# Chunk-selecting attention and a hardswish MLP on one core: the scheduler's slack, its mode charge and a new sequence of parts

## The chip, the cores and the metric

The kernel runs on one core of one Trainium2 chip. The metric is device time in microseconds of that core, from the first to the last instruction, as the median of several executions. The engines are PE (TensorE), DVE (VectorE), ACT (ScalarE), POOL (GpSimd) and SP (SyncE, which issues most of the DMA transfers).

## The reference, cut to what matters

```python
# attention: q, k, v are (4, 8, 768, 64) float32; chunks of 32 keys
k_min, k_max = min and max of k over each chunk
ub = sum_d max(q * k_min, q * k_max)           # an upper bound of the scores with a chunk
ub = where(causal chunk, ub, -1e9)
top = the 6 chunks with the largest ub, for each query
scores = where(in a top chunk and causal, q @ k.T / 8, -1e9)
attn = softmax(scores) @ v
# MLP on x = attn as (3072, 512); w_in (512, 2048), w_out (2048, 512)
h = x @ w_in
out = (h * clip(h + 3, 0, 6) / 6) @ w_out      # float32
```

## The kernel before

The attention is done for 16 pairs of heads, four pairs for each of the four batches. The MLP is done for 8 groups of 384 tokens, two for each batch. The work is cut into parts, each named by a token; one token often stands for an instruction group on PE and for what follows it on ACT or DVE:

- `k`, `q`, `v` (L281, L282, L290): loads of a pair's keys, queries and values. `w` (L302, L309): eight loads of quarters of the two weight matrices, issued by POOL. Each weight load waits for the cast of one pair's values, the pair that `WGATE` (L294) names, and for the weight load before it.
- `K`, `Q`: transposes of keys and queries on PE (L320), a copy out of PSUM on ACT (L335, L365), for keys the maximum and minimum over chunks on DVE (L339) and their difference (L347), for queries max(q, 0) on DVE (L369). `B`, `R`, `C`: casts to bf16 on POOL.
- `U`: the upper bounds on PE (L388) in 24 matmuls that use tiles of 64 x 32 of the array, and the addition of the causal bias on DVE (L396). `V`: their transpose (L410), the eight largest of each row (L418, twelve DVE instructions) and the comparison with the sixth (L421). `L`: the transpose of the selection (L438) and its copy out (L442).
- `S`, six for a pair: scores plus selection penalty on PE (L468, L473; tiles of 64 x 128), the exponential on ACT (L479) and the causal mask of the diagonal block on POOL (L483).
- `P`, two for a pair: probabilities times values on PE (L509), and the normalization on DVE (L514, L519).
- `X`: the attention's output transposed for the MLP; for batch 0 on PE (L557) with a DVE copy, for batches 1 to 3 by DMA transposes that SP issues (L546).
- `H`, eight for a group: eight matmuls with w_in (L578), relu on ACT (L582), minimum and product on DVE (L588). `O`: matmuls with w_out (L604, L625), a copy out on ACT (L610) and the store (L613).

The instructions are not written down in the order of these functions. The class `Plan` (L43) is a list scheduler that runs while the program is built. Each part has an engine, a duration, dependences and buffers in rings of fixed size. At each step every engine proposes one part (L95 to L108), the engine whose part starts earliest gets it, and the resulting order is the order in which all instructions are emitted. On the chip each engine then works through its own instructions in that order, so the planner's times matter only through the order that they give.

Two things decide what an engine proposes. The first is the time at which a part could start: the end of what it depends on plus a latency, or the time at which the engine is free, and on PE 0.095 us more (`SWITCH`) where the tile mode changes. Modes are 0 (whole array), 1 (`S`) and 2 (`U`). The second is the key of the part, its place in `SEQUENCE` (L134), where a lower place goes first:

```python
s = slack.get(eng, 0.0)
if mine is None or (at + s < mine[0]) or (at < mine[0] + s and op.key < mine[1].key):
    mine = (at, op)
```

With a slack of zero the second half of the condition is never true without the first, so the key has no say: the earliest part wins, and among equals the one that has been a candidate for longest. Before the change only PE has a slack, of 0.1 us (L686). The scores `S` of one pair also wait for all `S` of the pair before (L486), and PSUM allows three `S`, `H`, `K`, `Q` or `U` results at a time (ring `big`, L199).

Of the kernel before, what the change touches and what calls it, by code (L numbers as in the profile page):

```python
# [10 lines left out]
ACT = mybir.ActivationFunctionType  # L11
# [10 lines left out]

LAT = {"PE": 0.22, "DVE": 0.09, "ACT": 0.09, "POOL": 0.09, "LD": 2.0, "ST": 2.0}
SWITCH = 0.095


class Buf:
# [15 lines left out]
class Plan:  # L43
# [11 lines left out]
    def add(self, eng, dur, tok, fn=None, deps=(), take=(), use=(), chain=None, mode=0):  # L55
        deps = list(deps)
        if chain is not None:
            deps.append(self.last.get(chain))
        op = Op(eng, dur, tok, self.place(tok), fn, deps, take, use)
        op.mode = mode  # L60
        if chain is not None:
            self.last[chain] = op
        self.ops.append(op)
        return op
# [18 lines left out]
    def run(self, slack):  # L83
        cand = {}
        after = {}
        for op in self.ops:
            op.left = len(op.deps)
            for d in op.deps:
                after.setdefault(d, []).append(op)
            if not op.left:  # L90
                cand.setdefault(op.eng, []).append(op)
        order = []
        while any(cand.values()):
            best = None
            for eng, lst in cand.items():  # L95
                mine = None
                for op in lst:
                    r = self.ready(op)
                    if r is None:
                        continue  # L100
                    at = max(r, self.free[eng])
                    if eng == "PE" and op.mode != self.mode:
                        at += SWITCH
                    s = slack.get(eng, 0.0)
                    if mine is None or (at + s < mine[0]) or (at < mine[0] + s and op.key < mine[1].key):
                        mine = (at, op)
                if mine is not None and (best is None or mine[0] < best[0]):
                    best = mine  # L108
            if best is None:
                raise RuntimeError("no order")  # L110
            at, op = best
            cand[op.eng].remove(op)
            op.at, op.end = at, at + op.dur
            self.free[op.eng] = op.end
            if op.eng == "PE":
                self.mode = op.mode
            for b in op.take:
                b.slot = self.count[b.ring] % len(self.rings[b.ring])
                self.rings[b.ring][b.slot] = b
                self.count[b.ring] += 1  # L120
            for d in after.get(op, ()):
                d.left -= 1
                if not d.left:
                    cand.setdefault(d.eng, []).append(d)
            order.append(op)
        assert len(order) == len(self.ops)
        return order
# [4 lines left out]


SEQUENCE = """  # L134
H6.10 H7.14 Q10 H7.12 H7.4 P5.1 H3.6 P10.1 q15 P12.1 K9 S8.1 O6.1.8 v12 X7.2 O3.0.12 v0 H3.8 H6.14 q10 X3.2
S10.1 S11.1 K4 O3.0.4 R0 U4 L13 P10.0 U10 S9.0 P4.1 S6.4 S0.3 q14 L11 H6.0 Q15 O6.1.4 P9.1 Q5 O6.1.12 q0 v2
O3.2.0 S0.0 q2 P9.0 k10 H2.12 Q11 S5.1 V5 H7.0 S7.0 L0 X1.0 H2.14 V9 P8.0 K8 k14 H7.10 v9 H3.0 X2.1 H0.10 H3.4
v10 K0 q1 U3 S4.4 S13.1 R8 X3.1 R5 C7 H2.4 O1.2.12 C1 S0.5 S6.3 H2.10 O2.0.4 v13 K13 k1 K10 H6.12 B1 O6.0.12 R1
O4.1.0 O6.0.8 P6.0 H3.10 H1.14 X6.1 O7.0.8 O6.2.4 w5 H7.6 S12.0 V4 O6.0.0 O1.0.12 H0.14 O3.2.8 V10 B7 k9 Q14
O2.1.0 O4.2.8 H2.6 S9.3 R10 S8.5 P8.1 H0.6 S0.1 S2.1 L5 U0 H1.10 B3 S12.1 O1.0.8 K6 V2 U15 O3.1.4 C0 H1.12 K11  # L140
L4 P11.0 S0.4 S9.1 H0.0 k15 H4.0 O4.0.0 U2 Q2 P13.1 H0.2 w0 V12 H1.2 B4 U9 O0.0.12 H0.4 v3 O5.1.0 W0 S8.2 S10.2
Q8 X4.2 H0.12 H6.6 B9 O5.0.0 B15 k6 S2.2 L12 R3 P1.1 w6 X4.1 O1.1.12 O5.2.0 S7.2 k3 H6.4 W2 O4.0.12 q12 O4.1.12
q13 X3.0 S8.3 H3.12 L2 S11.4 v11 Q3 V1 S10.4 U5 O3.1.8 S14.5 O1.0.4 S6.2 L14 q7 C5 O7.1.12 k8 U8 k11 O4.1.8
O3.1.12 S14.0 O2.0.12 q8 S3.3 S6.0 Q12 Q1 S2.4 C13 P13.0 P7.0 S9.4 K1 H6.2 O1.2.4 v8 O1.1.8 V15 P15.1 O1.2.0 R12
H5.12 O5.1.12 H7.2 S5.0 v15 O2.0.8 O0.1.4 H2.2 X2.2 X1.2 X7.0 O7.1.8 k0 H2.0 R11 S11.0 S7.1 O7.2.12 B5 w7 H3.14
S1.3 S8.4 H7.8 X7.1 S14.3 S4.3 H4.8 S4.1 O4.0.4 S2.5 U6 B8 X5.2 S15.5 O2.2.0 k13 v6 S5.3 S7.5 q6 S8.0 S9.2 K15
v4 H1.8 H5.2 k2 q4 P0.1 U7 S5.4 v5 P7.1 O4.2.12 S6.5 v7 O3.1.0 O0.1.0 q5 P3.1 O1.2.8 O5.0.8 H0.8 S4.5 S7.4 S1.4
L7 V3 S3.1 O3.0.8 S1.1 V7 O0.1.12 S7.3 k7 B13 H5.10 S2.0 S3.0 P1.0 S11.5 U13 P11.1 O6.2.8 W1 V8 O4.2.4 P4.0 V13
S4.0 V11 O7.0.4 Q6 H2.8 B10 C15 k5 S13.0 X2.0 O0.0.0 U1 O2.2.8 U12 P6.1 O3.2.12 L8 L6 U14 O6.2.12 P14.0 S10.3 Q4
S5.5 S9.5 P2.0 K2 C8 w4 w3 O6.1.0 X6.2 V6 S14.1 O0.1.8 k4 S14.2 S10.0 R13 S6.1 U11 B12 P2.1 S5.2 O4.1.4 O3.0.0  # L150
S13.2 O2.1.8 P12.0 X5.1 C14 K12 O2.2.12 O2.1.12 L15 H1.6 H6.8 H3.2 L1 H5.0 K3 H4.4 V0 q11 H4.6 O2.1.4 v14 C6 L9
H4.10 O7.1.4 B6 S15.3 H4.2 C3 O6.2.0 S4.2 O7.2.0 H1.0 C10 O0.2.0 O7.1.0 X4.0 S0.2 C11 C2 B2 S11.3 O5.1.4 O4.0.8
w1 H5.14 S13.5 O6.0.4 P5.0 S10.5 S15.1 P14.1 O7.2.8 L3 K14 P0.0 H4.12 O5.1.8 R7 S12.4 S3.5 O2.0.0 S12.5 S12.3 R4
O0.0.4 K5 C9 S11.2 C12 O7.0.12 O4.2.0 S15.4 Q13 R9 R2 S12.2 O0.2.12 V14 O1.1.0 O3.2.4 S1.2 q3 X6.0 H4.14 R14 L10
B14 S3.2 R15 S3.4 B0 H1.4 X5.0 R6 q9 C4 Q0 S14.4 B11 w2 X0.0 v1 k12 H5.8 S1.5 H5.6 O1.1.4 O0.0.8 K7 P15.0 O0.2.4
O5.0.4 O5.2.4 S15.2 O5.2.8 S13.3 O1.0.0 S13.4 O0.2.8 S1.0 S15.0 O5.2.12 O2.2.4 O7.0.0 O5.0.12 Q9 H5.4 Q7 P3.0
S2.3 X0.2
"""
POS = {tok: n for n, tok in enumerate(SEQUENCE.split())}

# [6 lines left out]
def kernel(  # L167
# [21 lines left out]
    Q0 = TOPK * CH  # L189
# [11 lines left out]
    plan = Plan(rings, dict(PE=1.4, DVE=3.2, ACT=2.2, POOL=9.3, LD=0.3, ST=0.0), place)  # L201
    add = plan.add
# [88 lines left out]
                       take=[s["vs"]], chain="ldv")  # L291
        s["o_v"] = add("POOL", 0.86, f"C{i}", castv, deps=[s["ldv"]], take=[s["vb"]], use=[s["vs"]], chain="castv")

    WGATE = (0, 2, 1, 5, 6, 5, 6, 2)  # L294

    def plan_weights():
        wi = moe_w_in.rearrange("(k p) f -> p k f", p=P)
# [2 lines left out]
        for n in range(4):  # L300
            c = n * (DFF // 4)
            iss = add("POOL", 0.63, f"w{n}",  # L302
                      lambda c=c: nc.gpsimd.dma_start(WIN[:, :, c:c + DFF // 4], wi[:, :, c:c + DFF // 4]),
                      deps=[st[WGATE[n]]["o_v"]], chain="wi")
            iss.gate = n
# [13 lines left out]
        for j in range(NBLK):  # L319
            nc.tensor.transpose(T[:, j * P:(j + 1) * P], src.obj[:, j].rearrange("p e d -> p (e d)"), IDENT32[:])  # L320

    UDUR = 0.70

    def plan_K(i):
        s, tok = st[i], f"K{i}"
# [167 lines left out]
    norms = [[] for _ in range(B)]  # L493
# [39 lines left out]
    def plan_mlp(g, wdma):  # L533
        tok0 = g * GRP
        b = tok0 // S
        blk0 = (tok0 - b * S) // P
        xt, gt = Buf("xt"), Buf("gt")

        def do_xt():
            ops = []  # L540
            if b >= XDMA:
                for t in range(TPG):
                    def tr(t=t):
                        if t == 0:
                            new(xt, [P, TPG, KT_HID, P], BF16, "XT")
                        nc.sync.dma_start_transpose(xt.obj[:, t], xb[b].obj[:, blk0 + t, :])  # L546
                    ops.append(add("LD", 0.7, f"X{g}.{t}", tr, deps=norms[b] + ops[:1], take=[xt] if t == 0 else [],
                                   use=[xb[b]] if t == 0 else [xb[b], xt]))
                return ops
            for k0 in range(0, KT_HID, 2):  # L550
                ps = Buf("sm")

                def tr(k0=k0, ps=ps):
                    T = new(ps, [P, 2, GRP], BF16, "XTP")
                    for kk in range(2):
                        for t in range(TPG):
                            nc.tensor.transpose(T[:, kk, t * P:(t + 1) * P],  # L557
                                                xb[b].obj[:, blk0 + t, (k0 + kk) * P:(k0 + kk + 1) * P], IDENTB[:])

                def ev(k0=k0, ps=ps):  # L560
                    if k0 == 0:
                        new(xt, [P, TPG, KT_HID, P], BF16, "XT")
                    nc.vector.tensor_copy(xt.obj[:, :, k0:k0 + 2, :].rearrange("p t k s -> p k t s"),
                                          ps.obj[:].rearrange("p k (t s) -> p k t s", s=P))
                tok = f"X{g}.{k0}"
                o = add("PE", 0.35, tok, tr, deps=norms[b], take=[ps], use=[xb[b]], chain="XT")
                ops.append(add("DVE", 0.56, tok, ev, deps=[o] + ops[:1], take=[xt] if k0 == 0 else [],
                               use=[ps] if k0 == 0 else [ps, xt], chain="xev"))
            return ops
# [113 lines left out]
            plan_P(i, e)  # L683
    for b in range(B):
        plan_mlp_batch(b, wdma)
    order = plan.run(dict(PE=0.1))  # L686
    done_const = False
    for n, op in enumerate(order):
        if not done_const and op.eng not in ("LD",):
# [34 lines left out]
```

The softmax here doesn't subtract the row's maximum and nothing guards it: scores larger than these inputs give would overflow.

## Time and profile before

| | |
|---|---|
| time, median of three | 301.45 us (301.21 to 303.66) |
| span of the profiled execution | 300.2 us |
| busy share of ACT, DVE, POOL | 59%, 55%, 31% |
| mean granted clock of TensorE | 0.988 |
| moved by DMA | 32.20 MB, on average 107 GB/s |
| first matmul of the scores, of the MLP | 16.7 us, 60.5 us after the start |
| end of the last matmul to the end of the span | 3.8 us |

A line of the timeline gives the start, the time from the first start to the last end, the engine, the line of the code, what is written and read, and in square brackets idle time before it with what ended it. The ends of matmuls are modelled and overlap the next start, so durations on PE are best read from start to start.

### The profile page before, as it was taken

How to read it: one execution, taken by the hardware profiler on the slowest of the kernel's cores; microseconds unless marked ns; L12 is line 12 of the kernel's file. 1: busy time of each engine (PE TensorE's matmuls, PEld its weight loads, DVE VectorE, ACT ScalarE, POOL GpSimd, SP SyncE). 2: the span in 40 equal slices, each digit the busy share in tenths (PEclk: the TensorE clock that was granted, in tenths of full speed). 3: DMA queues.
4: the chain of work that ended last, by engine and by line, in shares of the span. 5: the costliest groups of instructions: out<-in, count | busy, mean ns of one | idle time of the engine just before them, and what ended most of it. 6: DMA issues, size and time to landing. Idle time of an engine off the chain costs nothing.

```text
span 300.2 us, 7214 instructions
## 1 busy us (share of the span) xinstructions
PE 287.3 (96%) x2948; PEld 178.4 (59%) x2970; DVE 163.6 (55%) x448; ACT 178.3 (59%) x219; POOL 92.5 (31%) x168
## 2 busy tenths in 40 slices
PE   7899999999999999999999999999999998999994
PEld 7657577765666556566555664566555654655444
DVE  4768887756669876236857461468421551625300
ACT  1557798987556358755766772565567832654311
POOL 8756776662106135531220342021133100000000
PEclk9959999999999999999999999999999999999999
DMA  9999999999507999762400005201011015001112
GB/s 172 218 185 217 203 210 193 220 196 198 89 0 184 243 228 206 156 134 68 107 35 3 35 12 130 72 0 37 13 60 37 2 31 144 2 1 71 37 70 71
DMA packets 92914, 32.20 MB, mean 107 GB/s; under 512 B 85584, under 2 KB 89936, under 8 KB 92880
## 3 DMA queue, kind: packets, MB, share of 16 engines
q1 hardware_dynamic: 87088, 27.14, 42.1%
q0 software_dynamic: 4224, 4.19, 8.8%
q10 hardware_dynamic: 1568, 0.39, 0.7%
q8 instruction: 23, 0.38, 0.6%
q14 instruction: 11, 0.09, 0.1%
HBM read 27.26 MB, written 6.29 MB: 112 GB/s over the span
## 4 chain that ended last, share of the span: by engine, by line
PE 82%; DVE 4%; ACT 4%; DMA 3%; SPq 2%; issue 2%; POOL 1%; ACTq 0%; DVEq 0%; POOLq 0%
PE HP L578 28%; PE OP L604 22%; PE PVP L509 8%; PE SPS L468 7%; PE SPS L473 5%; PE UBP L388 4%; PE QT L320 3%; PE KT L320 3%; ACT PT L479 2%; PE UBQ L410 2%; SPq L546 2%; DMA XT<-Xb 2%; DMA KS<-in_k_dram 1%; PE OP L625 1%; PE SLT L438 1%
## 5 line engine op out<-in xcount | busy, mean ns | idle before, releaser
L479 ACT ACTIVATE PT<-SPS 128x1024 bf16<-128x1024 f32 (+1 forms) x96 | 82.3, 924 | 18.7 <-PE SPS L473 15.2
L588 DVE SCALAR_TENSOR_TENSOR GT<-U,HP 128x768 bf16<-128x768 bf16 x64 | 60.8, 953 | 54.4 <-ACT U L582 49.3
L578 PE MATMUL HP<-XT,WIN 128*128 128x384 bf16 x512 | 86.0, 326 | 1.4 <-DMA XT<-Xb 1.0
L604 PE MATMUL OP<-WOUT,GT 128*128 128x512 bf16 x346 | 82.6, 379 | 1.6 <-issue 0.3
L582 ACT ACTIVATE U<-HP,THREE 128x768 bf16<-128x768 f32 x64 | 57.7, 901 | 33.4 <-PE HP L578 33.2
L578 PEld LDWEIGHTS <-WIN 128*128 128x128 bf16 x512 | 49.4, 98 | 35.1 <-issue 2.2
L483 POOL TENSOR_SCALAR_AFFINE_SELECT PT<-PT 128x256 bf16<-128x256 bf16 x96 | 38.6, 408 | 73.5 <-ACT PT L479 72.9
L604 PEld LDWEIGHTS <-GT 128*128 128x128 bf16 x368 | 34.4, 98 | 39.1 <-issue 1.7
L610 ACT ACTIVATE OT<-OP 128x512 f32<-128x512 f32 x23 | 13.7, 597 | 45.4 <-PE OP L604 43.6
L468 PE MATMUL SPS<-RHS,LHS 64*128 64x512 bf16 (+3 forms) x256 | 34.5, 315 | 1.4 <-ACT PT L479 1.3
L473 PE MATMUL SPS<-SELT,EM 64*128 64x288 bf16 (+6 forms) x384 | 32.8, 253 | 0.2 <-DVE SELT L442 0.2
L509 PEld LDWEIGHTS <-PT 128*128 128x128 bf16 x672 | 23.3, 98 | 4.5 <-issue 1.5
L473 PEld LDWEIGHTS <-EM 64*128 64x128 bf16 x384 | 18.9, 96 | 8.1 <-issue 1.1
L375 POOL CAST RHS<-QTS 128x768 bf16<-128x768 f32 x16 | 15.1, 951 | 26.7 <-ACT QTS L365 26.1
L514 DVE RECIPROCAL RINV<-PVP 128x6 f32<-128x6 f32 x32 | 6.1, 192 | 30.5 <-PE PVP L509 30.3
L468 PEld LDWEIGHTS <-LHS 64*128 64x128 bf16 x256 | 11.7, 95 | 14.2 <-issue 10.7
L354 POOL CAST LHS<-KTS 128x768 bf16<-128x768 f32 x15 | 12.6, 847 | 23.0 <-ACT KTS L335 22.8
L519 DVE TENSOR_TENSOR Xb<-PVP,RINV 128x384 bf16<-128x384 f32 x32 | 17.7, 555 | 0.9
L365 ACT COPY QTS<-QT 128x768 f32<-128x768 f32 x16 | 12.4, 802 | 6.6 <-PE QT L320 5.1
L339 DVE TENSOR_REDUCE KM<-KTS 128x24 f32<-128x768 f32 x15 | 13.9, 943 | 4.4 <-ACT KTS L335 4.3
L335 ACT COPY KTS<-KT 128x768 f32<-128x768 f32 x15 | 11.9, 807 | 5.2 <-PE KT L320 5.2
L320 PE MATMUL KT<-IDENT_114,KS 128*128 128x128 f32 x96 | 13.5, 284 | 0.5 <-DMA KS<-in_k_dram 0.3
(113 smaller groups left out, 233.6 us busy)
## 6 DMA issues: line engine op xcount, KB each, us to landing
VS<-in_v_dram SPq DMA_DIRECT2D x32, 192.0 KB, 4.6
KS<-in_k_dram SPq DMA_DIRECT2D x31, 192.0 KB, 4.5
QS<-in_q_dram SPq DMA_DIRECT2D x31, 192.0 KB, 4.5
out_dram<-OT SPq DMA_DIRECT2D x23, 256.0 KB, 2.0
WIN<-in_moe_w_in_dram POOLq DMA_DIRECT2D x4, 512.0 KB, 7.2
WOUT<-in_moe_w_out_dram POOLq DMA_DIRECT2D x4, 512.0 KB, 10.9
XT<-Xb SPq DMA_TRANSPOSE x18, 2.5
out_dram<-OT SPq DMA_DIRECT2D x2, 128.0 KB, 1.7
```

Of the source, the lines that this page charges most:

```text
L320: nc.tensor.transpose(T[:, j * P:(j + 1) * P], src.obj[:, j].rearrange("p e d -> p (e d)"), IDENT32[:])
L375: nc.gpsimd.tensor_copy(new(s["rhs"], [P, S], BF16, "RHS")[:], qts.obj[:])
L468: nc.tensor.matmul(T[:, e, c:c + hi - lo], lhsT=s["lhs"].obj[e * D:(e + 1) * D, j * P:(j + 1) * P], rhs=s["rhs"].obj[e * D:(e + 1) * D, lo ...
L473: nc.tensor.matmul(T[:, e, c:c + hi - lo], lhsT=EM[e * D:(e + 1) * D, h, j * P:(j + 1) * P], rhs=s["selt"].obj[e * D:(e + 1) * D, x:x + hi ...
L479: nc.scalar.activation(T[:, :, 0:w], sp.obj[:, :, 0:w], ACT.Exp, scale=scale)
L483: nc.gpsimd.affine_select(out=dv, in_=dv, pattern=[[0, 2], [1, P]], compare_op=A.is_ge, fill=0.0, base=0, channel_multiplier=-1)
L509: nc.tensor.matmul(T[:, qb, :], lhsT=t[:, e, c:c + P], rhs=fx(s["vb"])[:, e, j, :], start=(j == 0), stop=(j == qb))
L519: nc.vector.tensor_tensor(out=xb[b].obj[:, :, h * D:(h + 1) * D], in0=pv.obj[:, :, 0:D], in1=s[("ri", e)][:].to_broadcast([P, NBLK, D]), o ...
L578: nc.tensor.matmul(T[:, f, 0:GRP].rearrange("p (t s) -> p t s", s=P), lhsT=WIN[:, kt, (f0 + f) * P:(f0 + f + 1) * P], rhs=xt.obj[:, :, kt, ...
L582: nc.scalar.activation(new(u, [P, 2, GRP], BF16, "U")[:], hp.obj[:, :, 0:GRP], ACT.Relu, bias=THREE[:], scale=1.0)
L588: nc.vector.scalar_tensor_tensor(out=gt.obj[:, f0:f0 + 2, :], in0=u.obj[:], scalar=6.0, in1=hp.obj[:, :, 0:GRP], op0=A.min, op1=A.mult)
L604: nc.tensor.matmul(T[:, :], lhsT=gt.obj[:, f, t * P:(t + 1) * P], rhs=WOUT[:, f, :], start=(f == 0), stop=(f == FT - 1))
```

## The change

The scheduler's slack, which was for PE alone, is now given to ACT, DVE and POOL as well. With it, an engine may be held for up to 0.15 us for a part with a lower key, and among parts that could all start at once the key decides. The tile-mode charge is no longer made when PE leaves mode 2, and the duration of `U` falls from 0.70 to 0.60. The duration that the planner gives to the issue of a DMA transpose rises from 0.7 to 1.3. The pairs that gate the weight loads change, and all 496 places of the sequence are new. What is computed, and each instruction, stay the same; only their order changes.

```diff
+SLACK = dict(PE=0.1, ACT=0.15, DVE=0.15, POOL=0.15)
...
-                    if eng == "PE" and op.mode != self.mode:
+                    if eng == "PE" and self.mode not in (op.mode, 2):
                         at += SWITCH
...
 SEQUENCE = """
-H6.10 H7.14 Q10 H7.12 H7.4 P5.1 H3.6 P10.1 q15 P12.1 K9 S8.1 O6.1.8 v12 X7.2 O3.0.12 v0 H3.8 H6.14 q10 X3.2
...
+S4.4 H3.12 O1.1.12 R10 S2.2 V8 R11 W2 L6 U2 H6.14 P4.0 v8 X4.1 X3.2 S4.1 O2.1.8 P0.1 P2.1 R2 v9 S7.3 S6.3 P5.1
...
-    WGATE = (0, 2, 1, 5, 6, 5, 6, 2)
+    WGATE = (2, 3, 3, 0, 3, 4, 8, 7)
...
-    UDUR = 0.70
+    UDUR = 0.60
...
-                    ops.append(add("LD", 0.7, f"X{g}.{t}", tr, deps=norms[b] + ops[:1], take=[xt] if t == 0 else [],
+                    ops.append(add("LD", 1.3, f"X{g}.{t}", tr, deps=norms[b] + ops[:1], take=[xt] if t == 0 else [],
...
-    order = plan.run(dict(PE=0.1))
+    order = plan.run(SLACK)
```

Places in the two sequences of the parts that the prediction speaks of, counted from 0:

| parts | before | after |
|---|---|---|
| Q1, V0, K1, L0 | 213, 380, 219, 55 | 50, 113, 145, 183 |
| the eight P of pairs 0 to 3, mean | 332 | 160 |
| X0.0, X0.2 | 465, 495 | 234, 231 |
| all S, mean | 270 | 233 |
| all H, mean | 204 | 186 |
| all O, mean | 280 | 305 |

More of the change, by code (lines that the diff above doesn't have):

```diff
@@ L134 @@
 SEQUENCE = """
-H6.10 H7.14 Q10 H7.12 H7.4 P5.1 H3.6 P10.1 q15 P12.1 K9 S8.1 O6.1.8 v12 X7.2 O3.0.12 v0 H3.8 H6.14 q10 X3.2
[L136 to L154, printed above, removed]
@@ L155 @@
-B14 S3.2 R15 S3.4 B0 H1.4 X5.0 R6 q9 C4 Q0 S14.4 B11 w2 X0.0 v1 k12 H5.8 S1.5 H5.6 O1.1.4 O0.0.8 K7 P15.0 O0.2.4
-O5.0.4 O5.2.4 S15.2 O5.2.8 S13.3 O1.0.0 S13.4 O0.2.8 S1.0 S15.0 O5.2.12 O2.2.4 O7.0.0 O5.0.12 Q9 H5.4 Q7 P3.0
-S2.3 X0.2
+S4.4 H3.12 O1.1.12 R10 S2.2 V8 R11 W2 L6 U2 H6.14 P4.0 v8 X4.1 X3.2 S4.1 O2.1.8 P0.1 P2.1 R2 v9 S7.3 S6.3 P5.1
+U3 q1 V5 P8.0 S6.0 q12 L3 k5 S0.2 H2.2 S1.1 Q6 H1.8 H2.6 O7.0.4 S0.4 W1 S4.0 L4 O6.1.0 H5.14 O0.1.0 P12.0 B11
+P3.1 S3.0 Q1 Q10 H5.6 H6.6 S10.2 U12 Q9 K10 L1 H1.6 w6 O1.2.8 H3.4 H3.2 H0.10 H7.14 S10.0 Q5 H0.8 S10.5 L5
@@ new lines @@
+O0.0.12 X2.2 O1.2.12 S15.2 P12.1 H5.2 w3 S5.1 H0.4 S6.4 P1.1 P7.0 w0 O3.2.0 H2.4 O5.0.8 P5.0 P9.1 C7 C13 H3.8
+S5.2 C6 B10 X3.1 V4 V3 H6.2 P13.0 U5 S4.3 H7.4 H1.0 H1.4 Q4 O2.1.12 O1.2.4 H3.14 P15.1 P11.1 S13.0 k4 V0 O7.2.8
+H7.8 S8.3 S9.0 H2.12 O2.0.4 H0.12 S2.4 Q2 S9.2 H0.0 O3.0.12 O2.2.4 P3.0 S14.3 q14 k7 O1.1.8 L8 Q13 S9.4 R5 V10
+H2.8 S10.4 k2 S3.4 U0 K0 S13.1 X2.0 K1 H2.14 H3.10 H5.4 S1.2 C0 O2.0.8 B3 v4 P15.0 O6.0.4 U7 L11 q10 C9 k6 H5.8
+B8 w2 S9.1 K6 U10 S12.2 H5.0 R7 H4.10 W0 H6.4 P4.1 S6.2 B15 Q0 O2.2.0 S12.4 U6 S6.5 C11 O2.0.12 L0 H1.12 H1.2
@@ new lines @@
+H0.14 L13 k12 S4.2 S7.2 O0.0.0 S0.3 S9.3 O0.2.8 P10.1 q7 P9.0 O3.0.8 S7.1 v13 H6.8 U8 O1.0.0 S15.0 O2.2.12 L10
+H1.10 U4 O5.2.0 L14 S11.4 K8 S5.3 S0.0 X5.2 S4.5 S11.5 V9 k3 O1.1.0 L12 Q3 S6.1 O7.1.8 P14.1 H5.12 q0 k14 S7.4
+V6 X0.2 O5.0.12 O0.1.4 X0.0 w7 H6.10 C2 O7.0.8 S1.3 S7.0 V11 B6 H0.6 S11.2 H7.6 H4.0 S10.1 O3.0.4 O0.1.12 P8.1
+H3.0 S3.3 H1.14 S13.3 X1.0 R1 k8 S15.3 P2.0 Q8 S2.0 S0.5 O6.0.0 q5 X3.0 X2.1 O6.2.4 S11.0 O5.1.0 H2.0 X1.2 q13
+X5.0 Q11 v14 O4.1.8 K3 S13.5 S10.3 S1.4 P0.0 S1.0 S5.4 H5.10 S8.1 v7 R8 k0 S7.5 R3 q9 O5.2.12 K11 O2.2.8 K14 C3
@@ new lines @@
+q15 P6.1 Q7 B2 S2.1 R4 O4.0.4 H4.2 S1.5 S12.0 R13 O0.0.8 H0.2 H7.12 C14 w5 O4.2.4 S3.5 w4 O2.0.0 H6.12 v6 L15
+V13 K9 S8.2 O3.1.8 K5 S13.2 S8.0 O1.0.12 v5 V7 S11.1 S8.4 H7.10 O0.2.0 H4.12 O5.1.4 O7.1.0 v12 q4 V2 O5.2.4 H7.2
+V14 K4 X7.0 X5.1 Q14 U13 P10.0 B0 C4 H4.8 q2 B1 H3.6 B14 O6.0.12 S2.5 X4.2 S13.4 O3.1.0 k9 U9 O5.1.12 O5.0.0
+O3.1.12 S14.5 O5.2.8 B7 S12.1 O5.0.4 v3 O4.0.8 O7.2.12 H6.0 O4.2.12 L2 P11.0 O4.2.0 S9.5 U14 v0 S0.1 H7.0 O1.2.0
+v15 C12 S14.1 C15 R14 R12 R0 O4.0.0 S12.5 K7 H2.10 O0.0.4 S14.0 S15.5 P6.0 X7.1 v2 O3.2.8 C8 V15 B12 C1 S15.1
@@ L158 @@
+q11 R15 O0.2.4 O1.0.8 O2.1.0 S5.5 v11 R9 V1 S12.3 H4.14 O6.1.8 O7.0.12 O7.1.12 O4.1.4 Q15 S3.2 O4.2.8 w1 P13.1
+v1 k13 K15 O3.1.4 S8.5 O6.0.8 R6 K13 B13 O6.2.12 K12 L7 S14.2 O7.2.0 X6.2 C10 O0.2.12 H4.4 P7.1 X7.2 K2 O3.2.4
+P1.0 S3.1 B9 L9 B4 S2.3 B5 q3 O4.1.12 V12 S11.3 O1.1.4 O6.2.0 U11 P14.0 k10 C5 Q12 v10 O6.2.8 X6.1 S5.0 O6.1.4
+k11 O3.0.0 q6 U15 k1 O5.1.8 U1 k15 O7.0.0 X4.0 O2.1.4 S14.4 O7.1.4 O4.0.12 S15.4 O3.2.12 X6.0 O1.0.4 O4.1.0
+O0.1.8 q8 O6.1.12 H4.6
 """
```

## The prediction

> **What bounds the kernel now.** I read the page's busy shares and slices first, then PE's list of waits, then the timelines of PE and DVE at the places which these name, and the DMA issues last.
>
> ```profile
> PE 287.3 (96%) x2948; PEld 178.4 (59%) x2970; DVE 163.6 (55%) x448; ACT 178.3 (59%) x219; POOL 92.5 (31%) x168
> ...
> PE   7899999999999999999999999999999998999994
> ...
> PEclk9959999999999999999999999999999999999999
> DMA  9999999999507999762400005201011015001112
> ```
>
> PE is the bound from start to end: 96% busy, and every slice but the first, the last and one near 250 us is full. No other engine is above 59%. The clock shows one dip; by slices of half a microsecond it stands at 0.50 from 16.4 to 23.2 us. DMA is full for the first 75 us and mostly idle after.
>
> ```profile
> PE WRM L664 <- POOL IDENT_114 masks.py:199: 1.4, 1, 1.4
> PE SPS L468 <- ACT PT L479: 1.3, 4, 0.6
> PE HP L578 <- DMA XT<-Xb: 1.0, 1, 1.0
> PE SLT L438 <- DVE SEL_130 L421: 0.9, 1, 0.9
> PE QT L320 <- DMA QS<-in_q_dram: 0.8, 1, 0.8
> ```
>
> Columns: total us, times, longest. These are PE's largest idle times. With the small ones PE idles 9.0 us in all, summed over its instructions: 1.7 before and just after the warm-up matmuls, 2.0 between 10 and 17.5 us while the first pair's selection is made, 4.1 in some fifteen waits after 33 us, 1.2 in pieces under 80 ns. The last matmul ends 3.8 us before the span does. So a new order can win little from idle time. The other thing that an order sets on PE is how often the tile mode changes:
>
> ```profile
> 49.90 0.83 PE L509 MATMUL PVP<-VB_123,PT 128*128 128x65 bf16 x21
> 50.66 0.54 PE L388 MATMUL UBP<-QP,KC_128 64*32 64x192 f32 x12
> 51.01 0.52 PE L388 MATMUL UBP<-QTS,KC_128 64*32 64x192 f32 x12
> 51.46 0.84 PE L509 MATMUL PVP<-VB_123,PT 128*128 128x65 bf16 x21
> ```
>
> The 21 matmuls at 49.90 take 0.76 us to the next start, against 21 x 0.032 = 0.67 for their median start to start: the change into another mode costs 0.09. The 24 matmuls of one U take 0.80 (51.46 - 50.66), and two U in a row 1.48 (106.30 to 107.78): 0.68 for one and 0.12 for leaving. Walking down PE's timeline I count 115 changes of mode: 46 runs of S, and 13 runs of the 16 U. At about 0.095 each that is 10.9 us, within PE's busy time.
>
> ```profile
> 12.54 0.94 DVE L339 TENSOR_REDUCE KC_127<-KTS 128x24 f32<-128x768 f32 x1
> 13.40 1.16 DVE L418 MAX8 T_288<-UBQ 96x8 f32<-96x24 f32 x12
> 14.48 0.56 DVE L369 TENSOR_SCALAR QP<-QTS 128x576 f32<-128x576 f32 x1
> 14.96 0.17 DVE L347 TENSOR_TENSOR KC_127<-KM,KC_127 128x24 f32<-128x24 f32 x1
> 15.05 0.44 DVE L421 TENSOR_TENSOR SEL_130<-UBQ,T_288 96x288 bf16<-96x288 f32 x1
> ```
>
> This is the order that the planner now gives DVE while PE waits 0.94 us for SEL: the second pair's K work stands ahead of the first pair's selection.
>
> ```profile
> VS<-in_v_dram SPq DMA_DIRECT2D x32, 192.0 KB, 4.6
> ...
> WIN<-in_moe_w_in_dram POOLq DMA_DIRECT2D x4, 512.0 KB, 7.2
> WOUT<-in_moe_w_out_dram POOLq DMA_DIRECT2D x4, 512.0 KB, 10.9
> XT<-Xb SPq DMA_TRANSPOSE x18, 2.5
> ```
>
> The last column is us from issue to landing. The planner counts 3.1 for a weight load; four issued together (WOUT) took 10.9 in the median.
>
> **What the Trainium skill says.** "TensorEngine Tiling (Array Packing)", Key Properties: changing the tiling mode drains the array. The trace agrees, with 0.09 us into U and about 0.12 out of it; so leaving U isn't free. "TensorE: Matmul & The Clock Gate", Part 1: the clock is halved after a window of about 3.4 us with too little activity. The trace has one half-speed stretch, 6.8 us long, just after the waits at 13.8 and 15.5 us. "DMA: Bandwidth & Descriptors", Queues, rings and completion order: a DMA engine takes turns between the queues that have work. The trace agrees in kind: weight loads that overlap land later.
>
> **The change part by part.** No instruction is added or removed, so PE's work without the mode changes, 287.3 - 10.9 = 276 us, stays.
>
> *Mode charge and UDUR.* The planner's cost of a lone U falls from 0.095 + 0.70 + 0.095 = 0.89 to 0.095 + 0.60 = 0.695. Measured: 0.09 + 0.80 = 0.89. The old account was right, the new one is 0.2 short, 16 x 0.2 = 3.2 us in all. That costs nothing by itself, since PE works in written order and parts behind U slide; what waits for U is two parts later at the earliest. I take 0, with 0 to 0.5 as bounds.
>
> *Slack on DVE, ACT and POOL.* Before, the key had no say there. At 12.54 both the second reduction of K1 and the maxima of V0 can start; now V0 (place 113) beats K1 (145). The maxima then run 12.5 to 13.7, QP of Q1 (50) to 14.2, SEL to 14.6, and L0's transposes start at about 14.7 in place of 15.55. But the same reduction still stands ahead of U1 and of SELT: SELT ends near 15.9 and U1 starts there, as now at 15.79. PE's 0.94 us moves behind L0, and only the 0.16 before the first penalty matmuls (17.48) and a little more goes: -0.3. The same freedom acts where PE waits for ACT: at 230.25 it waited 0.63 for an exponential behind a copy of OT that had started at 228.61. A hold is at most 0.15 us and the engines have 40% and more to spare, so I count its cost at 0.
>
> *X from 0.7 to 1.3.* The trace has 1.26 us for one issue and 2.5 to the landing. The planner was 0.6 short for each of three in a row, and PE paid at 251.15 (1.01), at 243.05 (0.22) and at 188.15 (0.11). A truthful duration makes it start those transposes earlier or put O parts ahead of the H that needs them: 1.0 of the 1.34 goes.
>
> *Weights and sequence.* The order of the loads is a chain, so after the change one weight follows C2, four follow C3, one C4, two C8. In the trace C3 is cast at 39.0 us, C4 at 48.5 and C8 at 76.0. Six quarters are asked for before 50 us, where now three are. Their sources are 1.05 MB each, so 3.1 MB more compete with the pairs' loads. At the 205 GB/s of those slices that is 15 us of transfers. On the other side the P of pairs 0 to 3 and the X of group 0 move far up, so H, which PE can do without new pairs, begins before 60 us and can fill what late pairs leave open; and until C2 the first pairs have the DMA to themselves. I take 0 here, 0 to +4 as bounds.
>
> *The rest of the idle time.* Of 4.07 us after 33 us, 2.73 is not X. With three more engines ordered by key, half of it goes: -1.4 (bounds 0 and -2.7).
>
> *Mode changes.* Three result buffers allow runs of about three S: 96/3 = 32 runs in place of 46 would save 28 changes, 2.7 us. Ten runs more would cost 1.9. S moves up in the sequence (270 to 233) and O down (280 to 305), which speaks for S going as soon as a buffer is free and in longer runs. I take 10 changes fewer: -0.95.
>
> Sum: -0.3 - 1.0 - 1.4 - 0.95 = -3.65, so 301.45 - 3.65 = **297.8 us**.
>
> **The rivals.** *No change that counts:* the waits are only exchanged. For it: no wait after 33 us is longer than 1.0 us, and only the X item has a cause that the change plainly corrects. Against it: the tied choices on three engines were made without regard to what PE waits for. With X alone and half of the early item, 301.45 - 1.2 = 300.3 us.
>
> *Slower, transfers become the bound:* the clump behind C3 holds back pairs 4 to 7 while batch 0 isn't ready for H. For it: DMA is full until 75 us, and the planner's 4 x 3.1 = 12.4 us for four quarters are 4.2 MB/205 GB/s = 20 us, 8 us too few. Against it: the earlier H. If half of the 8 us shows on PE, 301.45 + 4 = 305.5 us.
>
> *The clock stays full:* if the early waits are spread otherwise, the half-speed stretch may not come: 6.8 x 0.5 = 3.4 us more, 294.4 us. For it: the stretch follows 1.7 us of waits between 13 and 16 us. Against it: by the working above as much waiting stays there.
>
> **How the numbers follow.** Forecast 0.42, full clock 0.12, no change 0.26, slower 0.20. Around each I allow 1.5 us, the width of the bounds on idle time and mode changes. The forecast lies just under the limit of 298.4, so a part of it counts as no change and a part of the no-change case as faster: faster 0.51, same 0.29, slower 0.20. The range from 293.3 to 304.3 leaves out about half of the slower case and a little of the full-clock case.
>
> **What would show it.** Right: PE's wait for the transposed X under 0.4 us, idle time of PE near 6 us, about 105 changes of mode, and PE's matmul work unchanged. The early item: L0's transposes at about 14.7 us. Wrong: waits of PE for KS or QS between 40 and 70 us, more runs of S than 46, a second half-speed stretch or none.

## The result, and the profile after

The changed kernel takes 309.78 us (median of four, 309.07 to 312.14) against 301.33 us before: a ratio of 1.0275, with a 95% interval of 1.0212 to 1.0339. The forecast was 297.8 us with a range of 293.3 to 304.3. The rival "slower, transfers become the bound" is what happened, and larger than the 305.5 us that I gave it.

The page of the changed kernel, busy shares and slices:

```profile
PE 285.2 (93%) x2949; PEld 178.1 (58%) x2970; DVE 164.1 (53%) x448; ACT 178.3 (58%) x219; POOL 91.8 (30%) x168
...
PE   7769984399999999999999999999999999999995
...
PEclk9999999689999999999999999999999999999999
DMA  9999999999848219993030000281000035100121
```

PE does the same work, but slices 7 and 8 (46 to 62 us) hold a hole that the kernel before doesn't have. After 75 us PE is full to the end. PE's list of waits (total us, times, longest) says what the hole waits for:

```profile
PE QT L321 <- DMA QS<-in_q_dram: 6.8, 2, 6.5
PE KT L321 <- DMA KS<-in_k_dram: 2.6, 2, 2.4
PE UBP L389 <- DVE UBT L397: 1.7, 1, 1.7
```

The wait for the transposed X, 1.0 us before, isn't in the list any more. The chain of waits around the hole (start, us, what) is one transfer:

```profile
40.90 0.21 PE SPS L474 x4
41.11 0.22 SPq L274
41.33 0.04 issue
41.37 17.21 DMA QS<-in_q_dram
58.59 0.14 issue
58.72 1.51 PE QT L321 x6
```

The queries of pair 7 took 17.2 us to land. The median of such a load is 4.6 us. POOL's timeline shows what was under way beside it:

```profile
36.57 0.82 POOL L289 CAST VB_123<-VS 128x768 bf16<-128x768 f32 x1
...
37.71 2.25 POOL L304 DMA_DIRECT2D WIN<-in_moe_w_in_dram  x3
...
40.30 0.78 POOL L311 DMA_DIRECT2D WOUT<-in_moe_w_out_dram  x1
...
46.74 0.76 POOL L311 DMA_DIRECT2D WOUT<-in_moe_w_out_dram  x1
```

C3 is cast at 36.57, and the four quarters that stand behind it go out within four microseconds, a fifth after C4. Their first use, the first H, is at 77.4 us; it was at 60.5 us before. SP, which issues the loads of pairs, is held up as well:

```profile
37.38 2.40 SPq L274 DMA_DIRECT2D KS<-in_k_dram  x2
39.88 4.69 SPq L274 DMA_DIRECT2D QS<-in_q_dram  x2
44.67 10.06 SPq L274 DMA_DIRECT2D VS<-in_v_dram  x2
54.83 3.85 SPq L274 DMA_DIRECT2D KS<-in_k_dram  x2
```

Between 40 and 59 us it issues the loads of little more than one pair. Two issues of values alone take 10 us.

The account in idle time of PE in the two profiled executions, summed over its instructions, in us:

| | before | after |
|---|---|---|
| 0 to 30 us | 3.8 | 6.5 |
| 30 to 45 | 0.7 | 1.1 |
| 45 to 75 | 0.6 | 9.7 |
| 75 to the end | 3.9 | 1.6 |
| mode changes | 115 | 112 |
| half-speed stretch, us from the start | 16.4 to 23.2 | 56.2 to 63.1 |
| last matmul to the end | 3.8 | 3.5 |

From 45 to 75 us it loses 9.1, and the half-speed stretch, which now falls on work that PE is bound by from 58.7 to 63.1, some 2.2 more (an estimate: half of these 4.4 us). After 75 us it wins 2.3. The early stretch and the early idle time turn out to trade against each other (below). With 0.4 from 30 to 45, and 0.7 won by mode changes and the tail, that is 9.1 + 2.2 - 2.3 + 0.4 - 0.7 = 8.7. The medians differ by 8.45 us and the spans of the two profiled executions by 7.4, so the account holds to about 1 us.

Not all idle time in this table is real. The traces hold 2948 and 2949 of the kernel's 2970 matmuls; all that are missing belong to `O`, and where one is missing a small gap, mostly of 0.05 us, is counted as idle. That is some 1.4 us of the 3.9 after 75 us and nearly all of the 1.6, so PE really goes from about 2.4 us to almost none there; the difference of 2.3 stands.

### The profile page after: what moved, and what is told of

It is laid out like the page before. It is cut to its first block, busy times and chain, and to the rows that moved or that the text cites. A ratio compares the mean times of both kernels' runs of the same rounds, so it can differ in the third digit from the quotient of the medians.

```text
span 307.6 us, 7210 instructions
## 1 busy us (share of the span) xinstructions
PE 285.2 (93%) x2949; PEld 178.1 (58%) x2970; DVE 164.1 (53%) x448; ACT 178.3 (58%) x219; POOL 91.8 (30%) x168
## 4 chain that ended last, share of the span: by engine, by line
PE 85%; DMA 7%; DVE 4%; issue 1%; ACT 1%; ACTq 0%; SPq 0%
PE HP L579 27%; PE OP L605 26%; DMA QS<-in_q_dram 7%; PE PVP L510 7%; PE SPS L469 7%; PE SPS L474 5%; PE UBP L389 4%; PE QT L321 3%; PE KT L321 3%; PE UBQ L411 2%; PE OP L626 1%; PE SLT L439 1%; ACT PT L480 1%; PE WRM L665 1%; DVE KM L340 1%
## 5 line engine op out<-in xcount | busy, mean ns | idle before, releaser
L611 ACT ACTIVATE OT<-OP 128x512 f32<-128x512 f32 x23 | 13.7, 596 | 43.5 <-PE OP L605 39.4
L474 PE MATMUL SPS<-SELT,EM 64*128 64x288 bf16 (+6 forms) x384 | 32.0, 251 | 0.0
L321 PE MATMUL QT<-IDENT_114,QS 128*128 128x128 f32 x96 | 13.9, 285 | 6.8 <-DMA QS<-in_q_dram 6.8
## 6 DMA issues: line engine op xcount, KB each, us to landing
WOUT<-in_moe_w_out_dram POOLq DMA_DIRECT2D x4, 512.0 KB, 10.2
```

What stands on the lines that cost most here:

```text
L474: nc.tensor.matmul(T[:, e, c:c + hi - lo], lhsT=EM[e * D:(e + 1) * D, h, j * P:(j + 1) * P], rhs=s["selt"].obj[e * D:(e + 1) * D, x:x + hi ...
```

## The experiments

Theory A says that the clump of weight transfers starves the loads that PE and POOL stand at in their written order. The rivals are named in the expectations: the new sequence issues loads too late whatever the weights do (B), or the slack and the price of U cost the time (C). All runs are against the kernel before on the same chip.

**Weights later, all else in the same order.** After the planner has run, five weight issues are taken out of the list and put back behind the casts named in the edit (`behind` does that); PE, DVE, ACT and SP keep their order.

```diff
     order = plan.run(SLACK)
...
+    order = behind(order, {'w1': 'C4', 'w2': 'C5', 'w3': 'C5', 'w4': 'C6', 'w5': 'C7'})
```

> The changed kernel with the order of every engine kept, except that POOL issues five of the eight weight quarters later (WIN 1 behind C4, WIN 2 and 3 behind C5, WOUT 0 behind C6, WOUT 1 behind C7; all were issued from 37.7 to 46.7 us). Theory A, the weight transfers starve the loads of pair 7, for which PE stands in its written order: the waits of 2.4 us for KS and 6.5 us for QS go, and with them the half-speed stretch that follows (some 2 us); 309.8 - 11 = about 299 us, with Q7 landing by about 50 us in place of 58.6. Theory B, the new sequence issues pair 7's loads too late whatever the weights do: 308 us or more, the waits stay. Theory C, the cost lies in the slack or in the price of U on other engines: no change from 309.8.

Measured: 299.26 us against 301.89, a ratio of 0.9899 (0.9841 to 0.9956). PE's waits in this run:

```profile
PE SLT L439 <- DVE SEL L422: 2.1, 4, 1.1
PE UBP L389 <- DVE UBT L397: 1.7, 1, 1.7
...
PE UBP L389 <- DVE KC L348: 1.2, 1, 1.2
...
PE KT L321 <- DMA KS<-in_k_dram: 0.3, 1, 0.3
```

The two long waits for loads are gone, and the half-speed stretch with them. Moving five instructions on POOL, which is 30% busy, is worth 10.5 us. B and C fall: the same sequence, slack and prices give 299 us. (The profile is of the slowest of the five executions, 300.98 us.)

**A smaller dose: only the two WOUT quarters later.**

```diff
+    order = behind(order, {'w4': 'C6', 'w5': 'C7'})
```

> The changed kernel with only the two WOUT quarters issued later (behind C6 and C7), the three WIN quarters stay at 37.7 to 39.2 us. A dose between the changed kernel and the one with all five late. Theory A: 2.1 of the 5.2 MB leave the stretch, about 10 us of transfers at 205 GB/s shared with the loads, so Q7 lands near 52 us and the waits of PE for KS and QS fall from 8.9 to 2 to 4 us; 301 to 304 us. Theories B and C: 308 to 310.

Measured: 305.02 us, 1.0113 (1.0072 to 1.0154), in between as expected, though above the 301 to 304 of theory A. The waits for KS are 3.1 us and those for QS 0.4; the longest load of queries takes 12.1 us in place of 17.2, and a half-speed stretch of 3.4 us follows in place of 6.8.

**The clump in the kernel before.**

```diff
     order = plan.run(dict(PE=0.1))
...
+    order = behind(order, {'w3': 'C3', 'w4': 'C3', 'w5': 'C4'})
```

> The kernel before with the order of every engine kept, except that POOL issues WIN 3 and WOUT 0 behind C3 and WOUT 1 behind C4, as the changed kernel does; they were issued from 58.4 to 64.3 us. In this order PE transposes pair 7 only at 89 us. Theory A needs both, early weights and an early pair 7: 301 to 303 us. Theory A', the early weights alone are enough, because the next loads are late whoever needs them: waits of PE for loads between 45 and 60 us, 306 to 310 us. Theory B: 301.4.

Measured: 308.85 us, 1.0230 (1.0192 to 1.0269). The narrow form of theory A, that an early pair 7 is needed as well, is wrong: A' holds. On POOL and on PE it looks so:

```profile
53.93 0.83 POOL L288 CAST VB<-VS 128x768 bf16<-128x768 f32 x1 [5.07 <-DMA VS<-in_v_dram]
...
55.47 1.85 POOL L483 TENSOR_SCALAR_AFFINE_SELECT PT<-PT 128x256 bf16<-128x256 bf16 x5
```

```profile
50.23 0.32 PE L509 MATMUL PVP<-VB,PT 128*128 128x65 bf16 x5
55.95 1.20 PE L509 MATMUL PVP<-VB,PT 128*128 128x65 bf16 x16 [5.40 <-POOL PT L483]
```

Here the values of a pair come late. POOL stands at their cast for 5.07 us, five masks that are due queue behind it, and PE waits 5.40 us for a mask. PE's list blames POOL; POOL's own line shows the DMA.

**Pair 7 later, the clump kept.**

```diff
     order = plan.run(SLACK)
+    late = [op for op in order[:next(k for k, op in enumerate(order) if op.tok == "V7")]
+            if op.tok in ("K7", "B7", "Q7", "R7", "U7", "K8", "B8", "Q8", "R8")]
+    order = [op for op in order if op not in late]
+    n = next(k for k, op in enumerate(order) if op.tok == "V7")
+    order[n:n] = late
```

> The changed kernel with the weights as early as they are, but with the parts K, B, Q, R of pairs 7 and 8 and U7 moved behind all that the planner put before V7 (K7 planned at 47.0, Q7 at 48.9, V7 at 64.7 us), so that PE has the scores and values of pairs 3 to 5 to do while pair 7 loads. Theory A: the two waits for KS and QS shrink from 8.9 us to 0 to 2, the half-speed stretch goes, 299 to 302 us. Theory A', the weights starve whatever is loaded: the wait moves to the values of pair 5 or to pair 8, 305 us or more. Theory C: no change.

Measured: 318.18 us, 1.0546 (1.0502 to 1.0590), worse than the changed kernel. The wait moved, as A' says, and again by way of POOL:

```profile
60.98 0.83 POOL L289 CAST VB<-VS 128x768 bf16<-128x768 f32 x1 [7.89 <-DMA VS<-in_v_dram]
61.76 2.22 POOL L484 TENSOR_SCALAR_AFFINE_SELECT PT<-PT 128x256 bf16<-128x256 bf16 x6
```

PE waits 6.09 us for the masks. Then the parts of pairs 7 and 8, now in a bunch from 71 to 84 us, wait for ACT and DVE among themselves, and 13.7 us at half speed come on top. It isn't a matter of which load PE stands at.

**The gates alone.** One constant is changed and the planner runs as in the changed kernel.

```diff
-    WGATE = (2, 3, 3, 0, 3, 4, 8, 7)
+    WGATE = (2, 3, 4, 5, 5, 7, 8, 8)
```

> The changed kernel with one line different: WGATE = (2, 3, 4, 5, 5, 7, 8, 8), so that one weight quarter follows each of C2, C3, C4, two follow C5, one C7 and two C8. The planner gives the same end for it, 295.6 us, since it charges each quarter 3.1 us on a queue of its own account. Theory A, the clump of weights is what costs: 298 to 301 us, no wait of PE above 1 us for KS or QS between 45 and 60 us. Rival, the gain of the version with hand-moved weights came from moving WIN 1 off C3 too: 302 to 304 us.

Measured: 299.96 us, 0.9932 (0.9907 to 0.9956). So, with this sequence, the WGATE line carries the whole loss. Apart from four of the weight issues, every engine has the same order as in the changed kernel, part for part, and the planner's own end is 295.6 us for both; on the chip they take 300.0 and 309.8. The profile is of the slowest of ten executions, 303.43 us, and shows a mild form of what the clump does:

```profile
PE PVP L510 <- POOL PT L484: 2.1, 1, 2.1
...
PE KT L321 <- DMA KS<-in_k_dram: 0.5, 1, 0.5
```

POOL stood for 2.76 us at a cast that waited for values, with the masks behind it.

**The price of the DMA transpose,** put back on top of that.

```diff
-                    ops.append(add("LD", 1.3, f"X{g}.{t}", tr, deps=norms[b] + ops[:1], take=[xt] if t == 0 else [],
+                    ops.append(add("LD", 0.7, f"X{g}.{t}", tr, deps=norms[b] + ops[:1], take=[xt] if t == 0 else [],
```

> The same with the planner's duration of a DMA transpose put back from 1.3 to 0.7. The planner then puts H6.0 at 247.5 in place of 252.4 us, right behind transposes that it believes to be done. If the price of the transpose is what removed PE's wait for the transposed X (my item of 1.0 us), that wait comes back with 0.5 us or more for a group and the time rises by 0.5 to 2 us over gates_spread. If it was the new sequence that removed it, there is no such wait and the time stays within 0.5 us.

Measured: 300.64 us, 0.9965 (0.9952 to 0.9979), 0.7 above gates_spread. PE doesn't wait for the transposed X here either: its idle time after 75 us is 0.06 us, in a trace in which no matmul is missing. There are 116 mode changes in place of 112, 4 x 0.095 = 0.4 us. So the transpose's price is worth a little at most (the two intervals overlap), and it isn't what removed the wait.

**The same price alone, in the kernel before.**

```diff
-                    ops.append(add("LD", 0.7, f"X{g}.{t}", tr, deps=norms[b] + ops[:1], take=[xt] if t == 0 else [],
+                    ops.append(add("LD", 1.3, f"X{g}.{t}", tr, deps=norms[b] + ops[:1], take=[xt] if t == 0 else [],
```

> The kernel before with the transposes' duration at 1.3 in place of 0.7 and nothing else. My item: PE's wait of 1.0 us for the transposed X at 251 us goes, 300.4 us. Rival: the old sequence was fitted to the old price, the planner's own end rises from 299.4 to 301.6 us, and the chip follows it, 303 to 304 us.

Measured: 301.39 us against 301.56, 0.9990 (0.9973 to 1.0006): no difference. The wait for the transposed X at 251 us is gone, but a wait of 1.0 us for a selection after 75 us and three more mode changes take its place. The planner's own end had risen by 2.2 us, which the chip doesn't follow.

**One held DVE instruction moved forward.**

```diff
+    u1 = next(op for op in order if op.tok == "U1" and op.eng == "DVE")
+    order.remove(u1)
+    order.insert([k for k, op in enumerate(order) if op.tok == "K2" and op.eng == "DVE"][1], u1)
```

> gates_spread with one DVE instruction moved: the bias addition of U1 ahead of the second reduction of K2, where the slack's key order (K2 448, U1 479) had put it behind. In the changed kernel PE waits 1.65 us at 19.5 us for it, since U2's result needs the buffer that it frees. If the hold is a loss of its own, that wait falls by over 1 us and the time by 1 to 1.6. If DVE bounds this stretch anyway (K2's difference, which U2 needs as well, comes half a microsecond later), nothing is won: within 0.5 us of gates_spread.

Measured: 300.06 us, 0.9937 (0.9913 to 0.9961), the same as gates_spread. PE's wait for the bias addition (1.7 us) goes, and that for the difference of K rises from 1.2 us to

```profile
PE UBP L389 <- DVE KC L348: 2.8, 2, 1.5
```

In this sequence DVE bounds the stretch; the order of its instructions shifts PE's wait from one of them to the other.

**Truthful prices and a new sequence.** Is the wrong price of the weight loads the root? With 5.1 us for a quarter the sequence of the change gives no order at all (the planner runs into a part that no buffer is left for), so a new sequence was sought for these prices, once with the gates of the change and once with the spread ones (the 496 new places are left out here).

```diff
-            res.append(add("LD", 3.1, "", None, deps=[iss], chain="w"))
+            res.append(add("LD", 5.1, "", None, deps=[iss], chain="w"))
...
-                    if eng == "PE" and self.mode not in (op.mode, 2):
+                    if eng == "PE" and op.mode != self.mode:
...
-    UDUR = 0.60
+    UDUR = 0.70
```

> The changed kernel with its gates and slack as they are, the planner's price of a weight quarter raised from 3.1 to 5.1 us (1.05 MB at the 205 GB/s of the trace), U and its mode charge as measured (0.70, charged on leaving too), and a sequence found anew for these prices, since the old one gives no order with them. The planner's end is 301.5 us; it now issues quarters at 37.1, 38.1, 43.5, 44.6 and 47.6 us and puts K7 at 51.4. If the wrong price is the root, a planner that knows it steers round the clump even with these gates: PE's waits for KS and QS between 45 and 65 us stay under 3 us in all, 300 to 304 us. If transfers that share the queues can't be planned as one after the other at all, the hole comes back: 307 us or more.

Measured: 308.50 us, 1.0217 (1.0170 to 1.0264), close to the rival's 307 and outside what the price theory allowed. The hole is smaller but there, with 10.2 us at half speed from 54.6 us on:

```profile
PE QT L320 <- DMA QS<-in_q_dram: 3.9, 1, 3.9
PE UBQ L410 <- DVE UBT L396: 2.6, 3, 2.3
```

Even with 5.1 us for a quarter the planner puts transfers one after the other. A load that went out ahead of the weights is done for it, while on the chip it shares the engines with what comes later. Here the load of queries that PE stood at was issued at 43.04 us, just ahead of weight quarters at 43.50, 44.63 and 47.22, and took 12.8 us. The better price for one transfer didn't repair that.

> The same prices with the gates 2, 3, 4, 5, 5, 7, 8, 8 and a sequence found for them; the planner's end is 299.5 us with 109 mode changes. 297 to 301 us: no wait above 1.5 us for loads after 30 us. If below 299 it is better than the version with weights moved by hand.

Measured: 301.07 us, 0.9975 (0.9947 to 1.0004): no hole, and no gain either. Its idle time after 75 us is 3.8 us, of which some 1.1 is missing matmuls, against the 0.06 of the sequence of the change.

**The price of U alone, in the kernel before.**

```diff
-                    if eng == "PE" and op.mode != self.mode:
+                    if eng == "PE" and self.mode not in (op.mode, 2):
...
-    UDUR = 0.70
+    UDUR = 0.60
```

> The kernel before with only the price of U changed as in the change (0.60, no charge on leaving) and its old sequence and gates. My item: the price costs nothing by itself, 301 to 303 us. Rival: the old sequence is fitted to the old prices; the planner's own end rises from 299.4 to 304.7 us although it counts 3.2 us less for the 16 U, and the chip follows, 305 us or more.

Measured: 309.77 us, 1.0255 (1.0220 to 1.0289). The rival holds. The wait for the transposed X grows to 3.1 us, that for the exponentials to 3.0, and PE's idle time after 180 us from 2.4 to 6.3. The planner's own end had risen by 5.3 us with the new price, and here the chip went the same way.

## Why the prediction was wrong

**What bounds the kernel, and the size of the gain.** PE as the bound was right, and the size of what the order could win was about right. With the weights out of the way the kernel is 2.6 us faster than before when they are moved by hand (299.26 against 301.89) and 1.6 us with the other gates (299.96 against 301.56), where my sum without the weights was 3.65.

**The step that failed: weights and sequence.** It said: "I take 0 here, 0 to +4 as bounds." The working ahead of it was right: four quarters behind C3, 3.1 MB more before 50 us, 15 us of transfers. What I set against it was wrong: that H "begins before 60 us and can fill what late pairs leave open". The first H ran at 77.4 us, and at 69.0 even where the weights were late and there was no hole. I had read it off the places of P and X in the sequence. A place decides only between parts that are ready within the slack, and batch 0 wasn't ready: its last scores, S3.1, stand right behind Q7 in the written order, and the planner itself had put H0.0 at 66 us, behind K7, Q7, K8 and Q8. With nothing to fill, the late load shows in full: 8.9 us of waits for KS and QS, and 2.2 us of half speed behind them, where the rival had taken half of 8 us.

The kernel before shows what filling looks like. It has a clump too, one quarter issued at 58.40 us and four more from 63.49, and a load of values beside them took 13.3 us:

```profile
63.49 2.99 POOL L310 DMA_DIRECT2D WOUT<-in_moe_w_out_dram  x4
```

```profile
60.52 5.36 PE L578 MATMUL HP<-XT,WIN 128*128 128x384 bf16 x32
...
68.37 5.37 PE L578 MATMUL HP<-XT,WIN 128*128 128x384 bf16 x32
```

PE has two runs of H in its order there, 10.7 us that need no new pair, and from 45 to 75 us it idles only 0.6 us. Three of these quarters moved forward in the same order, to 39.39, 40.14 and 54.70 us, where no H stands, cost 7 us (before_early_weights). So a clump of weights isn't a loss by itself; it is one where PE's order, or POOL's ahead of it, comes to a load before there is work to fill.

**The rest of the sum**, with the weights late, against the kernel before, in the profiled executions. *Idle time after 30 us*: 3.8 us without the gaps of missing matmuls (5.2 with them) to 3.1, so -0.7, where the X item and the rest together were -2.4. It is spread otherwise than I thought: after 75 us it falls from about 2.4 to 0.06 us, between 30 and 75 us it rises from 1.4 to 3.1. *X*: the wait went, but in the new sequence not for its price; at 0.7 it is gone too. Whether the new keys or the slack on the other engines removed it I can't say, since the new sequence gives no order without the slack on DVE, nor the old one with it; that remains open. *Early*: L0's transposes start at 13.14 us, even earlier than the 14.7 that I worked out, since both reductions of K1 gave way. But PE then waits 1.25 us at 16.0 and 1.65 at 19.5. From 12 to 30 us it idles 4.6 us, and 4.2 and 4.4 in the two runs with the old early order at full clock: -0.3 was +0.2 to +0.4. *Mode changes*: 3 fewer, not 10, so -0.3 and not -0.95. *Tail*: 0.4 us shorter, which I hadn't counted. Sum: -0.7 + 0.3 - 0.3 - 0.4 = -1.1, and the spans of the two profiled executions differ by -0.9. The medians differ by -2.6; the other executions with late weights were up to 2.3 us faster than the profiled one, and no profile shows where.

**Slips in reading the lines.** The scores stood in 49 runs, not 46 (the 115 mode changes are right); in the changed kernel there are 47. The 0.22 us at 243.05 wasn't a wait for a transpose: PE waited there for the normalization on DVE, and with the price of 1.3 in the old sequence it waits as before. Most of the 1.2 us "in pieces under 80 ns" are missing matmuls.

**Mode charge and UDUR, "0, with 0 to 0.5".** As a statement on the changed kernel it can't be isolated, since the new sequence gives no order with the old price. As a reason, that the price "costs nothing by itself", it was wrong: in the old sequence the price alone costs 8 us, through the order that it gives. That the sequence was fitted to the old price is my reading; a sequence sought for the new price in the kernel before wasn't tried.

**The full clock.** Falsified, with a reason worth keeping. In one set of 48 runs of the kernel before, 29 had a mean clock of 0.998 or more, with a median of 301.51 us. Of the other 19, at 0.987 to 0.997, one took 305.51 us and the rest have a median of 301.60. Only two of these have a clock as low as the profiled run's 0.988 (301.79 and 302.19 us), and where in a run the half-speed stretch lay is not on record; but a cost of 3.4 us would show, and it doesn't. The traces say why. From 12 to 30 us PE idles 1.9 us in the profile of before and 4.4 in x13_alone, which has the same early order and the full clock; 2.8 of these are waits for KS and QS and 1.2 for the selection on DVE. At half speed slower matmuls fill the time that PE otherwise waits for the loads. My 3.4 us for it counted half of 6.8 us as if PE had been the bound there.

**The chances.** The slower case had 0.20 and was worked out from the right cause. The range to 304.3 leaves out nearly all of it, not half: with 1.5 us around 305.5 it begins at 304.0. What should have raised the chance was in view: DMA full until 75 us, the planner's price of 3.1 us against a measured 7.2 to 10.9, and no evidence but places in a list for work that would fill the gap.

## What to carry to other kernels

When transfers are moved to an earlier time, ask first which loads they will share the DMA with, what stands behind those loads on each engine, and whether the order holds work there that needs none of them; a transfer that isn't needed for 40 us can cost 10 us by being early. Follow a wait past the engine that it names: PE's wait for POOL was POOL's wait for a load. And the end that a planner promises is worth no more than its model of the shared resource: two kernels with the same planned end differed by 10 us, while a planned difference of 2 us didn't show at all.

## What the runs showed of the hardware

A load of queries (192 KB) that lands in 4.5 us in the median took up to 17.2 us in the changed kernel beside five weight quarters, 12.1 us beside three (late_wout_only), and 10.3 us when the quarters were spread (late_weights). SP's issues stretched as well: two of them took 10.06 us in all where two typically take 1.5 to 2. The Trainium skill ("DMA: Bandwidth & Descriptors", Queues, rings and completion order) says that a DMA engine goes round the queues that have work; the runs agree that a second queue slows the first, and add by how much. A half-speed stretch of 6.8 us cost an estimated 2.2 us where PE was the bound for 4.4 us of it, while early in the kernel, where PE would have waited for loads and for DVE, the runs show no cost of it.
